# Gated mix of two attentions: 36 instead of 30 units on VectorE, seven operations each, and a bias column in ScalarE's exponential

## Chip, core and metric

The kernel runs on one core of a Trainium2 chip. The metric is the time of one execution on the device in microseconds; the time before is the median of three runs. Engines are named TensorE (PE), VectorE (DVE), ScalarE (ACT), GpSimd (POOL) and SyncE (SP) as in the profile.

## The reference

One sequence of 2048 tokens, 640 features, 32 heads of 20. Branch A is full softmax attention, branch B attends to 8 keys at distances 0, 2, ..., 14 back. A sigmoid gate of x mixes them. Both use the same x and have weights of their own.

```python
def _A_ref(x, wqkv, wo):            # 2048 keys for each query
    q, k, v = ...                   # 32 heads x 2048 x 20
    scores = einsum("bhqd,bhkd->bhqk", q, k) * 20 ** -0.5
    o = einsum("bhqk,bhkd->bhqd", softmax(scores), v)
    return merge_heads(o) @ wo

def _B_ref(x, wqkv, wo):            # 8 keys for each query
    kg, vg = k[..., idx, :], v[..., idx, :]     # idx = pos - 2 * (0..7)
    logits = einsum("bhsd,bhswd->bhsw", q, kg) * 20 ** -0.5
    attn = softmax(where(idx >= 0, logits, -1e9))
    o = einsum("bhsw,bhswd->bhsd", attn, vg)
    return merge_heads(o) @ wo

g = sigmoid((x * gate_w).sum(-1, keepdims=True))
return g * _A_ref(x, A_wqkv, A_wo) + (1 - g) * _B_ref(x, B_wqkv, B_wo)
```

Branch A has 32 x 2048 x 2048 exponentials, on 128 partitions 1,048,576 columns.

## The kernel before

**Units, steps and groups.** The work of branch A is cut into units of one head, one block of 128 keys (`kb`) and 512 queries: a score matmul of 32 rows into one PSUM bank of 128 x 512, an exponential, and a matmul with the values (`vA`, 21 columns, the first of which is one, so that the sum of the exponentials comes along). Four heads make a quad `q`, whose keys lie in `kT` and queries in `qT`, each head in 32 partitions. A quad and a block of 512 queries (`qc`) make a group of 64 units; there are 4 x 8 = 32 groups, numbered `gi`. Row 0 of each head's 32 is one in `kT` (from the column `e0`) and minus a bound on the scores in `qT` (`KM`, `qabs`), so the scores are already shifted when they come out of TensorE.

ScalarE takes its units in steps of three and two by turns, as wide as the PSUM banks 0 to 2 and 3 to 4 (`ST`): one instruction of 1536 or 1024 columns, line 1187, into one of six `ebuf`. Before it, TensorE has written the scores of the step (line 1172); after it, several steps' value matmuls run together (line 1195) into bank 5 (`OB`). At a group's end VectorE transposes that bank into `rg` (line 643) and normalizes it by the sums and the gate into `oTn` (lines 651 to 660).

**Units on VectorE.** A few units of each group (`XN`, at the places `XPOS`) never go to ScalarE. `gen_x` computes their exponential on VectorE, from a score matmul of its own (line 994): line 998 multiplies the score by `XMUL` and adds `XADD`, which makes a float whose integer value has the exponent of 2 in its upper bits; line 1002 clamps it and turns it into an integer; line 1003 takes the mantissa bits as a number between 1 and 2; lines 1004, 1006, 1007 and 1008 are a polynomial of it in the product form, and the last of them multiplies by the power of two that line 1005 cut out of the integer. `XADD` holds the logarithm of the polynomial's leading factor `XC4`. The three work tiles are `xb[0]`, `xb[1]` and `rg[0]`, the one that normalization uses, so a unit waits until the group before is normalized (`normdone`). Its result goes through a lone value matmul (line 1017) into bank 5.

**Other work.** The same five engines do all projections: keys (`gen_k`, line 412), queries (`gen_q`, lines 579 to 596, which first copies 80 columns of weights into `WqP`, line 382), values (`gen_v`). Branch B has three lanes: `gen_F` (lines 811 to 852) computes its queries, keys and products, `gen_K` (lines 866 to 966) its values, softmax and weighted sums, almost all on VectorE, with one small exponential on ScalarE per 512 queries (line 899); `gen_fold` and `gen_prefold` do the output projection. These lanes share the PSUM banks 6 and 7, which `take` and `give` hand around.

**What sets the order.** The order of the instructions on each engine is fixed when the program is built, by a planner at the end of `_build`. For each step `s` it places the step's exponential, the scores of step `s + 2`, the value matmuls when enough are pending, and in between pieces of the lanes. A lane is a generator that yields what it needs next ("pe", "dve", "dw" with a cost in ns, or "poll" until something holds); it has a window of steps in which it should proceed evenly, from `FWIN`, `KWIN`, `OWIN` in units of groups. A piece is placed if it fits into TensorE's and VectorE's planned time up to the step's end. A lane of group work that is not done in time is run to its end on the spot (`force`). Where TensorE would be left with little, filler matmuls are placed (lines 1314 and 1318). `task` records what each instruction reads and writes, and `emit` turns that into semaphore waits; each engine runs its list in order.

Of the kernel before, what the change touches and what calls it, by code (L numbers as in the profile page):

```python
# [5 lines left out]
FP32 = mybir.dt.float32  # L6
BF16 = mybir.dt.bfloat16
I32 = mybir.dt.int32
I16 = mybir.dt.int16
ALU = mybir.AluOpType  # L10
# [19 lines left out]
XC4 = 0.013534167746750096  # L30
XA = (-0.5785127719334512, 30.316837144955663, -17.76242689806009, 576.1803657752102)
XMUL = SCALE * 1.4426950408889634 * 2.0 ** 23
XADD = (127.0 + np.log2(XC4)) * 2.0 ** 23

XN = (0, 0, 1, 1, 1, 2, 2, 0, 1, 0, 0, 0, 0, 1, 2, 0, 0, 1, 1, 1, 1, 1, 0, 1, 2, 2, 1, 2, 1, 2, 1, 2)
FWIN = ((3.1, 4.4), (7.0, 11.7), (14.3, 18.8), (21.1, 25.7))
KWIN = ((6.3, 11.3), (6.0, 16.6), (15.3, 22.4), (24.3, 29.9))
OWIN = ((8.5, 12.7), (15.5, 20.2), (21.7, 25.8))
XPOS = ((7, 1), (9, 2), (5, 0))


class _Task:
# [202 lines left out]
def _build(ctx, nc, A_x, A_wqkv, A_wo, B_wqkv, B_wo, gate_w, out):  # L245
# [35 lines left out]
    zt = sb([P, P], BF16, "zt")  # L281
    Sel = sb([P, CN, 32], BF16, "Sel")
    e0 = sb([P, 1], FP32, "e0")
    KM = sb([P, NQUAD], BF16, "KM")
    Kmax = sb([P, 2, 5], FP32, "Kmax")
    WqP = [sb([P, CN, P], BF16, "WqP%d" % i) for i in range(2)]
    WkP = [sb([P, CN, P], BF16, "WkP%d" % i) for i in range(2)]
    kT = sb([P, NQUAD, S], BF16, "kT")
    vA = sb([P, NQUAD, KBN, 4 * VW], BF16, "vA")
    NQT = 3  # L290
    qT = [sb([P, 512], BF16, "qT%d" % i) for i in range(NQT)]
    qabs = sb([P, 512], BF16, "qabs")
    NEB = 6
# [2 lines left out]
    rr = [sb([P, 16], FP32, "rr%d" % i) for i in range(2)]  # L296
    rgn = [sb([P, 16, 32], BF16, "rgn")] * 2
    NOT = 14
    xb = [sb([P, 512], FP32, "xb%d" % i) for i in range(2)]
    oTn = sb([P, NOT, 512], BF16, "oTn")  # L300
    itmp = oTn[:, 10, 0:256].bitcast(I32)
    stmp = oTn[:, 11, 0:320].bitcast(I32).rearrange("p (c k) -> p c k", c=CN)
# [65 lines left out]
    T("pe", pe_warm, reads=["ident", "rgn"], writes=[("bk", 0)])  # L368
    T("dve", lambda e: e.memset(zt[:, :], 0.0), writes=["zt"])
    T("dve", lambda e: e.memset(e0[:, :], 0.0), writes=["e0"])  # L370
    for j in range(4):
        T("dve", lambda e, j=j: e.memset(e0[32 * j:32 * j + 1, :], 1.0), writes=["e0"])
    for i in range(2):
        T("dve", lambda e, i=i: e.memset(WkP[i][:, :, :], 0.0), writes=[("WkP", i)])
        T("dve", lambda e, i=i: e.memset(WqP[i][:, :, :], 0.0), writes=[("WqP", i)])

    T("dve", lambda e: e.memset(bank[OB], 0.0), writes=[("bk", OB)])

# [75 lines left out]
    def give(b, evac):  # L454
        held[b] = False
        if cur[0] is not None:
            cur[0].hold -= 1
        free_at[b] = evac.fin + 56.0
# [98 lines left out]

    def gen_q(gi):
        qc, q = divmod(gi, NQUAD)
        i = gi % 2  # L560
        yield ("dve", 370.0, 0.0)
        yield after(mk_wq(q, i))
        while ("KM", q) not in sch.bufs:
            yield ("poll",)
        b = yield from take()
        t = yield from chain(b, proj_mms(b, WqP[i], qc), [("WqP", i), "xT"])
        yield ("dw", t.fin, 690.0, 0.0)
        t = q_abs(b, gi)
        while ("KM", q) not in sch.bufs:
            yield ("poll",)  # L570
        yield ("t", max(t.fin, sch.bufs[("KM", q)][0].fin))
        yield ("pe", MM, 1.0)
        t = q_km(b, q)
        yield ("dw", t.fin, 690.0, 0.0)
        give(b, q_cp(b, gi))
# [402 lines left out]

    xdone = {}
    obstart = set()  # L980
    xA, xB, xC = xb[0], xb[1], rg[0]
    xe = xb[1][:, :].bitcast(BF16)[:, 0:512]

    def gen_x(gi, k, u):
        qc, q, kb, j = u
        while k > 0 and not xdone.get((gi, k - 1)):
            yield ("poll",)
        while gi > 0 and not normdone.get(gi - 1):
            yield ("poll",)
        A, B, C = xA[:, :], xB[:, :], xC[:, :]  # L990
        kA, kB_, kC = "xA", "xB", "rg"
        b = yield from take()
        yield ("pe", MM, 0.0)
        t = T("pe", lambda e: e.matmul(bank[b], kT[32 * j:32 * j + 32, q, kb * P:(kb + 1) * P], qT[gi % NQT][32 * j:32 * j + 32, :],  # L994
                                       start=True, stop=True),
              reads=[("kT", q, kb // 4), ("qT", gi % NQT)], writes=[("bk", b)], cost=MM)
        yield ("dw", t.fin, 690.0, 690.0)
        give(b, T("dve", lambda e: e.tensor_scalar(A, bank[b], float(XMUL), float(XADD), op0=ALU.mult, op1=ALU.add),  # L998
                  reads=[("bk", b)], writes=[kA], cost=690))
        Ai, Bi = A.bitcast(I32), B.bitcast(I32)  # L1000
        ops = [
            (430.0, lambda e: e.tensor_scalar(Ai, A, float(2 ** 23), None, op0=ALU.max), [kA], [kA]),
            (430.0, lambda e: e.tensor_scalar(Bi, Ai, 0x7FFFFF, 0x3F800000, op0=ALU.bitwise_and, op1=ALU.bitwise_or), [kA], [kB_]),
            (690.0, lambda e: e.scalar_tensor_tensor(C, B, XA[0], B, ALU.add, ALU.mult), [kB_], [kC]),
            (430.0, lambda e: e.tensor_scalar(Ai, Ai, 0x7F800000, None, op0=ALU.bitwise_and), [kA], [kA]),
            (690.0, lambda e: e.scalar_tensor_tensor(B, C, XA[2], B, ALU.add, ALU.add), [kC, kB_], [kB_]),
            (690.0, lambda e: e.scalar_tensor_tensor(C, C, XA[1], B, ALU.add, ALU.mult), [kB_, kC], [kC]),
            (690.0, lambda e: e.scalar_tensor_tensor(xe, C, XA[3], A, ALU.add, ALU.mult), [kA, kC], [kB_]),
        ]
        for c, fn, rd, w in ops:  # L1010
            yield ("dve", c, c)
            t = T("dve", fn, reads=rd, writes=w, cost=c)
        while (gi, j) not in obstart or (q, kb // 3) not in vdone:
            yield ("poll",)
        yield after(t)
        yield ("pe", MM, 0.0)
        T("pe", lambda e: e.matmul(bank[OB][32 * j:32 * j + DH + 1, :], vA[:, q, kb, VW * j:VW * j + DH + 1], xe, start=False,  # L1017
                                   stop=False, skip_group_check=True),
          reads=[kB_, ("vA", q, kb // 3)], accum=[("ob", j)], cost=MM)
        xdone[(gi, k)] = True  # L1020
# [163 lines left out]
    def mk_exp(s):  # L1184
        b0 = ST[s % 2][0]
        n = len(steps[s])
        return T("act", lambda e: e.activation(ebuf[s % NEB][:, 0:512 * n], ps[:, b0 * 512:(b0 + n) * 512], ACTF.Exp, scale=SCALE),  # L1187
                 reads=[("bk", b0 + i) for i in range(n)], writes=[("ebuf", s % NEB)], cost=ED[n])

    def mk_pv(s, us, cost):  # L1190

# [158 lines left out]
    for s in range(NS):  # L1350
# [4 lines left out]
        if first:  # L1355
            ng = gi + 1
            if ng < QCN * NQUAD:
                nqc, nq_ = divmod(ng, NQUAD)
                g_end = gstep(gi + 1)
                if nqc == 0:  # L1360
                    if nq_ % 2 == 1 and nq_ < NQUAD - 1:
                        p = (nq_ + 1) // 2
                        vl[p] = lane(gen_v(p), "v%d" % p, s + (20 if s == 0 else 2), gstep(gi + 2) + 8, 16.0)
                    ql[ng] = lane(gen_q(ng), "q%d" % ng, s + 4, g_end - 8 - lead(ng), 6.0, 2 if s == 0 else 1)
                else:
                    ql[ng] = lane(gen_q(ng), "q%d" % ng, s + 2, g_end - 10, 6.0, 0)
            n = len(xunits[gi])
            for k in range(n):
                sa, sb_ = s + 6, gstep(gi + 1) - 6
                xl[(gi, k)] = lane(gen_x(gi, k, xunits[gi][k]), "x%d.%d" % (gi, k), sa + k * (sb_ - sa) // n,  # L1370
                                   sa + (k + 1) * (sb_ - sa) // n, 4740.0, 0)
        E = mk_exp(s)
        odd = s % 2 == 1
        block[0], block[1] = False, 0.0
# [79 lines left out]
        while moved or not relaxed[0]:  # L1454
            relaxed[0] = not moved
            moved = False
            for g in sorted(lanes, key=lambda g: (g.hold == 0, g.s1 if g.name[0] in EAGER else INF)):
                if not g.done and g.due(s):
                    hot = g.name[0] in EAGER
                    lag = g.total * min(1.0, (s + 1 - g.s0) / max(1, g.s1 - g.s0)) - g.spent  # L1460
                    n = 0
                    while True:
                        lp = lim_pe
                        if npv[0] and not (hot and s >= g.s1):
                            lp = -INF
                        elif not hot and lag < 0.06 * g.total and block[1] >= SOFT:
                            lp = -INF
                        if not ready(g, s, lp, lim_dve):
                            break
                        moved = True  # L1470
                        n += 1
                        if not g.due(s) or (n >= 2 and not hot):
                            break
            for g in lanes:
                if g.done and not g.name.startswith("norm"):
                    ends.append((g.name, s, g.s1, round(g.spent, 1), g.total))
            lanes[:] = [g for g in lanes if not g.done]
# [65 lines left out]
```

## Time and profile before

| | |
|---|---|
| median of three runs | 949.87 us (949.42 to 951.07) |
| the profiled execution | 951.03 us |
| its span, first to last instruction | 949.2 us |
| mean granted TensorE clock | 0.996 |
| first exponential of line 1187 starts | 20.53 us |
| last one starts | 940.0 us |
| VectorE units: instructions of lines 998, 1002 to 1008 | 30 each, 141 us in all |
| normalization's transpose, line 643, waits for TensorE | 54.8 us |

The profile is one execution. Its busy times are the union of an engine's instructions, so overlapping instructions count once there, while the mean duration of a group is that of one instruction with its overlap. A line of the groups reads: line, engine, operation, output and inputs by name, shapes, count; then busy us and mean ns; then the idle time of the engine just before them, and what ended it. A row of the windows has, after the window and its length, the busy us of PE, its weight loads, DVE, ACT and POOL, with their counts, the granted TensorE clock, the DMA share and GB/s.

The span is a start of 20 us (loads, transposes of x, the first projections), the stream of exponentials of 921 us, and an end of 8 us with the last group's normalization and output.

### The profile page before, as it was taken

The numbers are of one execution on the slowest core, as the hardware profiler recorded it, in microseconds if no ns is written. First come the engines' busy times: TensorE is split into PE (matmuls) and PEld (weight loads), VectorE is DVE, ScalarE is ACT, GpSimd is POOL, SyncE is SP. The second block draws the span as 40 slices with busy tenths as digits, with TensorE's granted clock in tenths as the row PEclk, the third lists the DMA queues.
The fourth block names the chain that finished last, engine by engine and source line by source line (L and its number), as shares of the span: only waits on it lengthen the run. The fifth ranks groups of instructions, "written<-read, shape, count | busy, mean of one in ns | idle before, by whom it ended". The sixth has DMA issues, their size and how long they took to land.

```text
span 949.2 us, 16591 instructions
## 1 busy us (share of the span) xinstructions
PE 867.3 (91%) x6359; PEld 285.5 (30%) x6359; DVE 699.9 (74%) x1294; ACT 930.3 (98%) x833; POOL 3.1 (0%) x7
## 2 busy tenths in 40 slices
PE   8999999999889899999889899898899999899997
PEld 5333323232222222333222223322222333222232
DVE  5486665775688878668788876688898578898735
ACT  5999999999999999999999999999999999999997
POOL 1000000000000000000000000000000000000000
PEclk9999999999999999999999999999999999999999
DMA  9000000000000000000000000000000000000000
GB/s 311 9 1 20 17 1 1 1 22 15 1 1 2 1 1 1 1 15 8 8 1 1 1 1 8 9 14 1 1 2 1 8 9 15 1 2 1 1 1 29
DMA packets 12033, 12.86 MB, mean 14 GB/s; under 512 B 3380, under 2 KB 11316, under 8 KB 11956
## 3 DMA queue, kind: packets, MB, share of 16 engines
q1 hardware_dynamic: 9844, 11.43, 3.8%
q8 instruction: 52, 0.85, 0.4%
q10 hardware_dynamic: 2112, 0.37, 0.2%
q14 instruction: 25, 0.20, 0.1%
HBM read 9.18 MB, written 2.62 MB: 12 GB/s over the span
## 4 chain that ended last, share of the span: by engine, by line
ACT 68%; issue 16%; PE 15%; DVE 1%; DMA 1%; SPq 0%; ACTq 0%; DVEq 0%
ACT ebuf L1187 67%; PE ps L1172 5%; PE ps L400 4%; PE ps L1314 2%; PE ps L1195 2%; DMA x_tm<-in_A_x_dram 1%; PE ps L1039 1%; PE ps L483 0%; ACT L_sb L899 0%; PE ps L994 0%; DVE Kmax L1070 0%; PE ps L926 0%; PE ps L886 0%; PE ps L826 0%; PE ps L1017 0%
## 5 line engine op out<-in xcount | busy, mean ns | idle before, releaser
L1187 ACT ACTIVATE ebuf<-ps 128x1536 bf16<-128x1536 f32 (+1 forms) x807 | 915.6, 1358 | 2.2 <-PE ps L1172 1.0
L1172 PE MATMUL ps<-qT,kT 32*128 32x512 bf16 x2048 | 318.6, 382 | 66.0 <-ACT ebuf L1187 56.7
L1172 PEld LDWEIGHTS ps<-qT,kT 32*128 32x128 bf16 x2048 | 88.3, 91 | 345.5 <-issue 149.7
L1195 PE MATMUL ps<-ebuf,vA 128*21 128x512 bf16 x2018 | 170.7, 382 | 0.0
L1314 PE MATMUL ps<-xT,ident 128*128 128x512 bf16 x272 | 105.5, 388 | 6.7
L956 DVE TENSOR_TENSOR bw<-vB,bw 128x640 f32<-128x640 bf16 x112 | 91.9, 820 | 2.1
L960 DVE TENSOR_TENSOR blkacc<-blkacc,bw 128x640 f32<-128x640 f32 x96 | 78.9, 822 | 2.4
L842 DVE TENSOR_TENSOR prod<-qk 128x512 bf16<-128x512 bf16 x160 | 57.9, 418 | 15.8 <-PE ps L826 15.5
L1195 PEld LDWEIGHTS ps<-ebuf,vA 128*21 128x21 bf16 x2018 | 41.8, 90 | 72.3 <-issue 49.4
L400 PE MATMUL ps<-xT,WqkB 128*128 128x512 bf16 x200 | 63.5, 385 | 0.0
L643 DVE STREAM_TRANSPOSE rg<-ps 128x512 f32<-128x512 f32 x31 | 22.2, 717 | 54.8 <-PE ps L1195 54.8
L400 PE MATMUL ps<-woA_r,oTn 128*128 128x320 bf16 x240 | 48.5, 302 | 0.0
L1314 PEld LDWEIGHTS ps<-xT,ident 128*128 128x128 bf16 x272 | 26.0, 96 | 71.8 <-PE ps L1314 46.1
L400 PE MATMUL ps<-xT,WqP 128*128 128x512 bf16 (+1 forms) x165 | 47.2, 384 | 0.1
L400 PE MATMUL ps<-xT,WkP 128*128 128x512 bf16 (+1 forms) x165 | 46.1, 381 | 0.0
L579 DVE CAST qT<-ps 128x512 bf16<-128x512 f32 x31 | 21.4, 691 | 33.1 <-PE ps L400 33.0
L412 DVE TENSOR_SCALAR kT<-ps,e 128x512 bf16<-128x512 f32 x28 | 20.9, 748 | 28.8 <-PE ps L400 28.7
L400 PE MATMUL ps<-xT,WvB 128*128 128x512 bf16 x100 | 31.7, 384 | 0.0
L998 DVE TENSOR_SCALAR xb<-ps 128x512 f32<-128x512 f32 x30 | 20.7, 688 | 14.7 <-PE ps L994 9.9
L400 PE MATMUL ps<-WvA,oBacc 128*128 128x320 bf16 x160 | 31.3, 301 | 0.0
L596 DVE CAST qT<-ps 128x512 bf16<-128x512 f32 x31 | 21.3, 688 | 13.2 <-PE ps L589 13.1
L483 PE MATMUL ps<-WvA,xT 128*128 128x160 bf16 (+1 forms) x320 | 29.7, 233 | 0.0
(121 smaller groups left out, 653.0 us busy)
## 6 DMA issues: line engine op xcount, KB each, us to landing
x_tm<-in_A_x_dram SPq DMA_DIRECT2D x3, 640.0 KB
out_dram<-outsb SPq DMA_DIRECT2D x12, 160.0 KB
WqkB<-in_B_wqkv_dram SPq DMA_DIRECT2D x1, 1600.0 KB
WqkA<-in_A_wqkv_dram SPq DMA_DIRECT2D x2, 700.0 KB
qk<-in_B_wqkv_dram SPq DMA_DIRECT2D x1, 800.0 KB
woA_r<-in_A_wo_dram SPq DMA_DIRECT2D x32, 25.0 KB
WvA<-in_B_wo_dram SPq DMA_DIRECT2D x5, 160.0 KB
x_tm<-in_A_x_dram SPq DMA_DIRECT2D x2, 320.0 KB
```

The source lines that it names most:

```text
L400: ins = e.matmul(o, l, r, start=(k0 + k == 0), stop=(k0 + k == n - 1))
L483: ins = e.matmul(bank[b][:, i_ * wn:(i_ + 1) * wn], xT[:, c, kb * P:(kb + 1) * P], WvA[:, c, w0:w0 + wn], start=(c == 0), stop=(c == CN - 1))
L579: T("dve", lambda e: e.tensor_copy(qt[:, :], bank[b]), reads=[("bk", b)], writes=[("qT", gi % NQT)], cost=690)
L596: return T("dve", lambda e: e.tensor_copy(qT[gi % NQT][:, :], bank[b]), reads=[("bk", b)], writes=[("qT", gi % NQT)], cost=690)
L643: return T("dve", lambda e: e.transpose(rg[i][:, :], bank[OB]), reads=[("ob", j) for j in range(4)], writes=["rg"], cost=720)
L842: t = T("dve", lambda e, r=r, f=f, off=off: e.tensor_tensor(prod[r][:, :], qB[:, f, :], kB[:, f, off:off + 512], ALU.mult), reads=["qB", " ...
L956: T("dve", lambda e, vv=vv, av=av: e.tensor_tensor(tmpB, vv, av, ALU.mult), reads=[("aT", ai), "vB4"], writes=["tmpB"], cost=822)
L960: T("dve", lambda e: e.tensor_tensor(blkacc[:, :, :], blkacc[:, :, :], tmpB, ALU.add), reads=["tmpB"], writes=["blkacc"], cost=822)
L1172: ins = e.matmul(bank[b0 + i], kT[32 * j:32 * j + 32, q, kb * P:(kb + 1) * P], qT[gi % NQT][32 * j:32 * j + 32, :], start=True, stop=True)
L1187: return T("act", lambda e: e.activation(ebuf[s % NEB][:, 0:512 * n], ps[:, b0 * 512:(b0 + n) * 512], ACTF.Exp, scale=SCALE), reads=[("bk" ...
L1195: ins = e.matmul(bank[OB][32 * j:32 * j + DH + 1, :], vA[:, q, kb, VW * j:VW * j + DH + 1], ebuf[s % NEB][:, i * 512:(i + 1) * 512], start ...
L1314: T("pe", lambda e: e.matmul(bank[b], ident[:, :], xT[:, 0, 0:512], start=True, stop=True), reads=["xT", "ident"], writes=[("bk", b)], cos ...
```

## The change

It does seven things.

- The VectorE exponential has seven operations. The first one clamps the score from below at `XMIN` and multiplies it by `XMUL`, straight into an integer tile. Line 1002 goes. Without the addition the exponent's offset of 127 is missing; the mask that cuts out the exponent bits gets an exclusive-or with 0x40000000 as second operation, which puts it back up to a factor of two.
- The constant that `XADD` held is put on the other side: line 1187's exponential gets a bias, the column `xlog`, 128 x 1 in SBUF, filled with `ln(2 / XC4)`, so ScalarE's units carry the same factor as VectorE's; it cancels in the normalization.
- A third tile `xb[2]` takes the place of `rg[0]`. Room for it comes from `WqP` (one instead of two) and `qT` (two instead of three).
- A unit no longer waits for the previous group's normalization, but for all earlier units and for the end of its own group's query projection. Its lane's window begins seven steps before its group.
- `XN` has 36 units instead of 30, in other groups, up to three in one (`XPOS` has a fourth place).
- The windows of branch B's and the output's lanes are other numbers.
- In the planner's inner loop a lane of VectorE units ("x") or of `gen_K` ("K") gives way after each piece, so these two alternate.

```diff
-XADD = (127.0 + np.log2(XC4)) * 2.0 ** 23
-XN = (0, 0, 1, 1, 1, 2, 2, 0, 1, 0, 0, 0, 0, 1, 2, 0, 0, 1, 1, 1, 1, 1, 0, 1, 2, 2, 1, 2, 1, 2, 1, 2)
...
-XPOS = ((7, 1), (9, 2), (5, 0))
+XMIN = -126.0 / (SCALE * 1.4426950408889634)
+XLOG = float(np.log(2.0 / XC4))
+XN = (1, 2, 0, 2, 0, 2, 1, 2, 0, 0, 0, 0, 0, 1, 2, 1, 1, 0, 0, 3, 0, 2, 1, 1, 2, 2, 3, 1, 1, 1, 2, 2)
+FWIN = ((3.5, 2.1), (8.7, 7.6), (13.9, 21.4), (20.8, 24.3))
+KWIN = ((7.6, 8.5), (9.5, 12.4), (12.6, 24.7), (24.0, 23.4))
+OWIN = ((6.1, 13.1), (13.7, 23.5), (15.7, 31.2))
+XPOS = ((7, 1), (9, 2), (5, 0), (11, 3))
...
+    xlog = sb([P, 1], FP32, "xlog")
-    WqP = [sb([P, CN, P], BF16, "WqP%d" % i) for i in range(2)]
+    WqP = [sb([P, CN, P], BF16, "WqP")]
-    NQT = 3
+    NQT = 2
-    xb = [sb([P, 512], FP32, "xb%d" % i) for i in range(2)]
+    xb = [sb([P, 512], FP32, "xb%d" % i) for i in range(3)]
+    T("dve", lambda e: e.memset(xlog[:, :], XLOG), writes=["xlog"])
...
-    xA, xB, xC = xb[0], xb[1], rg[0]
+    xA, xB, xC = xb
-        while k > 0 and not xdone.get((gi, k - 1)):
+        while not all(xdone.get((g, i)) for g in range(gi + 1) for i in range(XN[g] if g < gi else k)):
-        while gi > 0 and not normdone.get(gi - 1):
+        while gi > 0 and not (gi in ql and ql[gi].done):
...
-        give(b, T("dve", lambda e: e.tensor_scalar(A, bank[b], float(XMUL), float(XADD), op0=ALU.mult, op1=ALU.add),
+        give(b, T("dve", lambda e: e.tensor_scalar(Ai, bank[b], float(XMIN), float(XMUL), op0=ALU.max, op1=ALU.mult),
-            (430.0, lambda e: e.tensor_scalar(Ai, A, float(2 ** 23), None, op0=ALU.max), [kA], [kA]),
-            (430.0, lambda e: e.tensor_scalar(Ai, Ai, 0x7F800000, None, op0=ALU.bitwise_and), [kA], [kA]),
+            (430.0, lambda e: e.tensor_scalar(Ai, Ai, 0x7F800000, 0x40000000, op0=ALU.bitwise_and, op1=ALU.bitwise_xor), [kA], [kA]),
...
-        return T("act", lambda e: e.activation(ebuf[s % NEB][:, 0:512 * n], ps[:, b0 * 512:(b0 + n) * 512], ACTF.Exp, scale=SCALE),
+        return T("act", lambda e: e.activation(ebuf[s % NEB][:, 0:512 * n], ps[:, b0 * 512:(b0 + n) * 512], ACTF.Exp, bias=xlog[:, 0:1],
+                                               scale=SCALE),
...
-                        if not g.due(s) or (n >= 2 and not hot):
+                        if not g.due(s) or (n >= 2 and not hot) or g.name[0] in "xK":
```

More of the change, by code (lines that the diff above doesn't have):

```diff
@@ L32 @@
 XMUL = SCALE * 1.4426950408889634 * 2.0 ** 23
-XADD = (127.0 + np.log2(XC4)) * 2.0 ** 23
-XN = (0, 0, 1, 1, 1, 2, 2, 0, 1, 0, 0, 0, 0, 1, 2, 0, 0, 1, 1, 1, 1, 1, 0, 1, 2, 2, 1, 2, 1, 2, 1, 2)
-FWIN = ((3.1, 4.4), (7.0, 11.7), (14.3, 18.8), (21.1, 25.7))
-KWIN = ((6.3, 11.3), (6.0, 16.6), (15.3, 22.4), (24.3, 29.9))
-OWIN = ((8.5, 12.7), (15.5, 20.2), (21.7, 25.8))
-XPOS = ((7, 1), (9, 2), (5, 0))
+XMIN = -126.0 / (SCALE * 1.4426950408889634)
[5 more added lines that the diff above has]
+XPOS = ((7, 1), (9, 2), (5, 0), (11, 3))
 class _Task:
@@ L374, in _build @@
         T("dve", lambda e, i=i: e.memset(WkP[i][:, :, :], 0.0), writes=[("WkP", i)])
-        T("dve", lambda e, i=i: e.memset(WqP[i][:, :, :], 0.0), writes=[("WqP", i)])
+    T("dve", lambda e: e.memset(WqP[0][:, :, :], 0.0), writes=[("WqP", 0)])
     T("dve", lambda e: e.memset(bank[OB], 0.0), writes=[("bk", OB)])
@@ L559, in gen_q @@
         qc, q = divmod(gi, NQUAD)
-        i = gi % 2
+        i = 0
         yield ("dve", 370.0, 0.0)
@@ L985, in gen_x @@
         qc, q, kb, j = u
-        while k > 0 and not xdone.get((gi, k - 1)):
+        while not all(xdone.get((g, i)) for g in range(gi + 1) for i in range(XN[g] if g < gi else k)):
             yield ("poll",)
-        while gi > 0 and not normdone.get(gi - 1):
+        while gi > 0 and not (gi in ql and ql[gi].done):
             yield ("poll",)
         A, B, C = xA[:, :], xB[:, :], xC[:, :]
-        kA, kB_, kC = "xA", "xB", "rg"
+        kA, kB_, kC = "xA", "xB", "xC"
         b = yield from take()
@@ L997, in gen_x @@
         yield ("dw", t.fin, 690.0, 690.0)
-        give(b, T("dve", lambda e: e.tensor_scalar(A, bank[b], float(XMUL), float(XADD), op0=ALU.mult, op1=ALU.add),
+        Ai, Bi = A.bitcast(I32), B.bitcast(I32)
+        give(b, T("dve", lambda e: e.tensor_scalar(Ai, bank[b], float(XMIN), float(XMUL), op0=ALU.max, op1=ALU.mult),
                   reads=[("bk", b)], writes=[kA], cost=690))
-        Ai, Bi = A.bitcast(I32), B.bitcast(I32)
         ops = [
-            (430.0, lambda e: e.tensor_scalar(Ai, A, float(2 ** 23), None, op0=ALU.max), [kA], [kA]),
             (430.0, lambda e: e.tensor_scalar(Bi, Ai, 0x7FFFFF, 0x3F800000, op0=ALU.bitwise_and, op1=ALU.bitwise_or), [kA], [kB_]),
             (690.0, lambda e: e.scalar_tensor_tensor(C, B, XA[0], B, ALU.add, ALU.mult), [kB_], [kC]),
-            (430.0, lambda e: e.tensor_scalar(Ai, Ai, 0x7F800000, None, op0=ALU.bitwise_and), [kA], [kA]),
+            (430.0, lambda e: e.tensor_scalar(Ai, Ai, 0x7F800000, 0x40000000, op0=ALU.bitwise_and, op1=ALU.bitwise_xor), [kA], [kA]),
             (690.0, lambda e: e.scalar_tensor_tensor(B, C, XA[2], B, ALU.add, ALU.add), [kC, kB_], [kB_]),
@@ L1186, in mk_exp @@
         n = len(steps[s])
-        return T("act", lambda e: e.activation(ebuf[s % NEB][:, 0:512 * n], ps[:, b0 * 512:(b0 + n) * 512], ACTF.Exp, scale=SCALE),
-                 reads=[("bk", b0 + i) for i in range(n)], writes=[("ebuf", s % NEB)], cost=ED[n])
+        return T("act", lambda e: e.activation(ebuf[s % NEB][:, 0:512 * n], ps[:, b0 * 512:(b0 + n) * 512], ACTF.Exp, bias=xlog[:, 0:1],
+                                               scale=SCALE),
+                 reads=[("bk", b0 + i) for i in range(n)] + ["xlog"], writes=[("ebuf", s % NEB)], cost=ED[n])
     def mk_pv(s, us, cost):
@@ L1366, in _build @@
                     ql[ng] = lane(gen_q(ng), "q%d" % ng, s + 2, g_end - 10, 6.0, 0)
[L1367 to L1371, printed above, removed]
+            for g_ in ((0, 1) if s == 0 else (gi + 1,)):
+                if g_ < QCN * NQUAD:
+                    n = len(xunits[g_])
+                    sa, sb_ = (6 if g_ == 0 else gstep(g_) - 7), gstep(g_ + 1) - 6
+                    for k in range(n):
+                        xl[(g_, k)] = lane(gen_x(g_, k, xunits[g_][k]), "x%d.%d" % (g_, k), sa + k * (sb_ - sa) // n,
+                                           sa + (k + 1) * (sb_ - sa) // n, 4310.0, 0)
         E = mk_exp(s)
```

## The prediction

> **What bounds the kernel now.** I read the busy table of the page first, then the groups by form, then the first microseconds of ScalarE's timeline, then TensorE's windows. The page:
>
> ```profile
> PE 867.3 (91%) x6359; PEld 285.5 (30%) x6359; DVE 699.9 (74%) x1294; ACT 930.3 (98%) x833; POOL 3.1 (0%) x7
> ...
> L1187 ACT ACTIVATE ebuf<-ps 128x1536 bf16<-128x1536 f32 (+1 forms) x807 | 915.6, 1358 | 2.2 <-PE ps L1172 1.0
> L1172 PE MATMUL ps<-qT,kT 32*128 32x512 bf16 x2048 | 318.6, 382 | 66.0 <-ACT ebuf L1187 56.7
> ```
>
> ScalarE is busy 98% of the span, 915.6 us of it in the 807 exponentials of line 1187, and it stood idle only 2.2 us in front of them. TensorE waits 56.7 us for those exponentials. So the end is set by one thing: the number of ScalarE exponentials times what each adds to an unbroken stream. VectorE (74%) is not on that path.
>
> ScalarE's groups by form:
>
> ```profile
> L1187 ACT ACTIVATE ebuf<-ps 128x1536 bf16<-128x1536 f32 x404 | 635.1, 1572 | 0.7 <-PE ps L1172 0.3
> L1187 ACT ACTIVATE ebuf<-ps 128x1024 bf16<-128x1024 f32 x403 | 461.1, 1144 | 1.5 <-PE ps L1172 0.7 <-ACT ebuf L1187 0.2
> ...
> L1066 ACT ACTIVATE kT<-ps,e 128x512 bf16<-128x512 f32 x3 | 2.1, 687 | 3.0 <-DVE Kmax L1070 2.3 <-PE ps L400 0.6
> ...
> L1049 ACT ACTIVATE xT<-ps 128x512 bf16<-128x512 bf16 x2 | 1.2, 594 | 1.4 <-PE ps L1039 1.4
> ```
>
> Two things stand here. 512 more columns cost 1572 - 1144 = 428 ns, 0.836 ns a column. And the inputs: line 1187 reads only ps, line 1066 reads ps and e, the bias column e0 in SBUF. At 512 columns the instruction with a bias column lasts 687 ns, the plain copy 594.
>
> **Part one: 30 units become 36.** A unit is one head, 128 keys, 512 queries. ScalarE keeps 2048 - 36 = 2012 units: in the changed program's instruction list 402 exponentials of 1536 columns and 403 of 1024, against 404 and 403. A duration is not what an exponential adds, since neighbours overlap (635.1 + 461.1 is more than 915.6). From the first exponential's start (20.53 us) to the last one's end (941.43) are 920.9 us; 2018 x 512 columns at 0.836 are 863.7, the four local softmax exponentials (line 899) about 3.4, which leaves 53.8 us over 812 activations, 66 ns each, the 2.2 us of idle included. So each 1536-wide exponential adds 1284 + 66 = 1350 ns, and two fewer give 2.7 us. This lies wholly on the path: -2.7.
>
> **Part two: a bias in the remaining 805.** Before, the bias of line 1187 is the number 0 inside the instruction; after, it is the column xlog in SBUF. No exponential of the trace has that, but line 1066 does, and once two of them follow each other directly. ScalarE's timeline there, and two plain copies in a row:
>
> ```profile
> 13.69 1.51 ACT L1049 ACTIVATE xT<-ps 128x1024 bf16<-128x1024 bf16 x2 [0.21 <-PE ps L1039]
> ...
> 18.58 1.05 ACT L1066 ACTIVATE kT<-ps,e 128x512 bf16<-128x512 f32 x2 [2.34 <-DVE Kmax L1070]
> ```
>
> In the trace's nanoseconds the copies run 13,691 to 14,715 (1024 columns) and 14,612 to 15,204 (512): the second one's end is 489 after the first one's, 61 more than its 428 of columns. With the bias column they run 18,578 to 19,265 (512) and 19,165 to 19,632 (256): 367 end to end, 153 more than its 214. The second was free to start: the VectorE reduction that it waits for ended at 18.82. The price is 153 - 61 = 92 ns by ends; by starts it is 159 (587 - 428) against 65 (921 - 856), 94. I take 93, since this is the nearest row: same engine, PSUM source, back to back, bf16 out. 805 x 93 = 74.9 us, with nothing to hide it, because ScalarE has no idle to give.
>
> Bounds for it: the lowest visible price compares Identity with the exponential itself, 687 - 428 = 259 fixed against 1043 - 856 = 187 for the first 1024-wide exponential, 72 ns, 58 us. The highest takes starts of the pair, 159, against the first two exponentials' starts (1331 - 1284 = 47), 112 ns, 90 us. Zero is a rival below.
>
> The Trainium skill speaks against this edit: ScalarE: Activation LUTs, section "What ACT_TABLE_LOAD costs", says that each per-partition pointer operand adds about 93 ns to an ACTIVATE. By that the sum is the same 74.9, and the pair above agrees; that exponentials in a long stream pay it is shown by no run here.
>
> **Part three: VectorE.** The first operation now clamps and multiplies PSUM into int32. No row has just that; line 998 (688 ns, PSUM to f32) and line 1002 (427, f32 to int32 in SBUF, as fast as line 1003's int32 to int32 at 424) bound a conversion at about nothing. Line 1002's operation goes, and the mask of line 1005 gets a second operation, for which 1003 with two (424) against 1005 with one (418) says +6. A unit costs 688 + 424 + 689 + 424 + 684 + 689 + 688 = 4.29 us instead of 4.71: 36 x 4.29 - 30 x 4.71 = +13 us of VectorE, under an engine with 249 us idle, stretched further by part two. On the path: 0; if the cover went it would be at most these 13. TensorE gets six more lone score and value matmuls; its 312 fillers (lines 1314, 1318) become 282, so it has room: 0.
>
> **Part four: waits and placement.** A third buffer lets a unit start before the previous group's normalization has read rg. One WqP and two qT instead of two and three: the copy into WqP (375 ns) waits for the projection one group, some 29 us, earlier, and qT's writer for scores two groups back, both long over. VectorE runs in order, so a unit whose score matmul is late holds up what stands behind it: projection copies, which feed qT, which feeds TensorE's next scores. That wait was 14.7 us over 30 units in front of line 998, 0.5 each, and it cost ScalarE nothing. The alternation with the local branch changes order only, and its work lies inside the same VectorE idle. 0, with a few us for the range. A memset for xlog and one fewer for WqP: 0.
>
> **Sum** against the profiled execution's span: 949.2 - 2.7 + 74.9 = 1021.4. What lies around the span was 1.8 us in that run (951.03); the median, 949.87, stands 0.7 over its span. So 1022.1 as a median; I say 1022.
>
> **Rivals.** First, the other side: the fetch of the bias column is hidden in a long stream, because the next exponential is issued while the last one runs (durations grow from 1457 for the first to 1572 on average with no change in pace, so the queue gets deeper). It decides if the whole 93 ns fits into that lead; then only part one is left, 949.87 - 2.7 = 947.2, faster. From about 3 ns exposed (2.7 us over 805) the change gains nothing. Against it: in the pair, which was free to overlap, neighbours overlap by 100 ns (19,265 - 19,165), the copies by 103, so the fetch was not absorbed. Chance 0.10.
>
> Second, TensorE's clock. TensorE's windows:
>
> ```profile
> 280.00:284.00 4.00, 2.47 (x19) 0.66 (x17) 3.90 (x7) 4.00 (x5) 0.00 (x0) 1.00 0.00 0
> 284.00:288.50 4.50, 4.50 (x20) 0.96 (x17) 2.04 (x4) 3.48 (x4) 0.00 (x0) 0.62 0.02 4
> ```
>
> After 4 us at 62% busy the granted clock fell to 0.62 of full in the next 4.5 us, and ScalarE lost 0.74 + 0.28 us of idle, about 1.4 with the late start. The Trainium skill, TensorE: Matmul & The Clock Gate, "Why this matters for your kernels", asks for idle gaps over about 3 us before the clock drops; by it nothing happens here. The row differs: the longest gap in that stretch was 0.92. A longer exponential thins TensorE's work by 8%. Cut into 3.4 us stretches, the length of the slowed one in the clock's records, the trace has TensorE below 0.78 busy in seven of 276 besides the start, and one of the seven was followed by the slow clock; six more at 1.4 us give 1022 + 8 = 1030. Chance of a loss of that kind, above 1026: 0.12.
>
> Third, VectorE's denser order leaves scores late: group 19 carries three units, 12.9 us in one 29 us group beside the local branch. One unit late by its own length costs 4.3 us; three, 13: 1035. For it: VectorE is busy 88 of 115 us between 487 and 602, where that group lies. Against it: between 602 and 717 it is busy 99 of 115 and ScalarE still all 115, and the slower stream gives 9 us more in such a stretch. Chance 0.03.
>
> **How the numbers follow.** Exposed price at about its size: 0.75, 1022, between 949.9 - 2.7 + 58 = 1005 and 949.9 - 2.7 + 90 = 1037. Hidden 0.10; clock 0.12; VectorE 0.03. The range 1006 to 1036 takes in nearly all but the hidden case. A change under 0.2% (1.9 us) can't be told from none here: faster 0.09, within 0.01 (a price of about 3 ns), slower 0.90.
>
> **What would show it.** Exponentials some 93 ns longer by pace: a pair of 1536 and 1024 taking about 2.45 us instead of 2.26 from end to end; ScalarE still 98% busy with about 990 us in the exponentials; the busy shares of TensorE and VectorE down to about 84% and 70%; TensorE's wait for ScalarE well above 56.7 us. If the pace stays at 2.26 the hidden rival holds and this forecast is wrong. If ScalarE's idle in front of its exponentials exceeds 5 us, clock windows or late VectorE work took it.

## The result and the profile after

The changed kernel takes 1023.25 us (median of four runs, 1019.07 to 1024.88) against 949.64 for the kernel before: 1.0767 times, 95% interval 1.0732 to 1.0802. The profiled execution took 1023.27 us with a span of 1021.5, 72.3 more than before. The ratios here and below leave out a single execution, of the kernel with a column of zeros, that took 3843.23 us where the others took 1021.

The busy table and the costliest groups of the changed kernel (line 1189 is the old 1187, line 1174 the old 1172):

```profile
PE 880.7 (86%) x6337; PEld 288.1 (28%) x6337; DVE 705.9 (69%) x1306; ACT 998.0 (98%) x831; POOL 3.1 (0%) x7
...
L1189 ACT ACTIVATE ebuf<-ps,xlog 128x1536 bf16<-128x1536 f32 (+1 forms) x805 | 984.1, 1501 | 7.8 <-PE ps L1174 7.5
L1174 PE MATMUL ps<-qT,kT 32*128 32x512 bf16 x2050 | 323.1, 386 | 126.5 <-ACT ebuf L1189 116.7
```

ScalarE is still the bound at 98%. It works 984.1 us for 805 exponentials where it worked 915.6 for 807, and TensorE waits twice as long for it (116.7 us, 56.7 before). The input list now reads ps,xlog. New is the end of that line: ScalarE stood idle 7.8 us in front of exponentials, 2.2 before, and nearly always until TensorE had written the scores.

ScalarE's groups by form:

```profile
L1189 ACT ACTIVATE ebuf<-ps,xlog 128x1536 bf16<-128x1536 f32 x402 | 689.2, 1714 | 2.5 <-PE ps L1174 2.4
L1189 ACT ACTIVATE ebuf<-ps,xlog 128x1024 bf16<-128x1024 f32 x403 | 518.3, 1287 | 5.2 <-PE ps L1174 5.1
```

An exponential lasts 142 or 143 ns more. That is not its price, as neighbours overlap. Eight of them in a row, four of each width, before and after, without a wait between them:

```profile
399.44 9.26 ACT L1187 ACTIVATE ebuf<-ps 128x1536 bf16<-128x1536 f32 x8
400.02 10.07 ACT L1189 ACTIVATE ebuf<-ps,xlog 128x1536 bf16<-128x1536 f32 x8
```

They take 0.81 us more, some 100 ns each, and the longer duration of the first is still in it. The price itself is read from end to end, over the whole trace: the median exponential of 1536 columns ends 1432 ns after the one before it, of 1024 columns 1005 ns; in the kernel before, 1344 and 917. So 88 ns each, 805 x 88 = 71 us. Less the columns, at 0.833 ns each, that is 152 ns now and 64 before.

The waits have a place. ScalarE's timeline and the windows at one of five such places:

```profile
326.62 9.11 ACT L1189 ACTIVATE ebuf<-ps,xlog 128x1536 bf16<-128x1536 f32 x7
336.55 1.11 ACT L1189 ACTIVATE ebuf<-ps,xlog 128x1024 bf16<-128x1024 f32 x1 [0.83 <-PE ps L1174]
338.49 1.54 ACT L1189 ACTIVATE ebuf<-ps,xlog 128x1536 bf16<-128x1536 f32 x1 [0.82 <-PE ps L1174]
```

```profile
329.50:333.00 3.50, 2.32 (x17) 0.70 (x17) 2.41 (x7) 3.50 (x4) 0.00 (x0) 1.00 0.00 0
333.00:340.00 7.00, 6.59 (x26) 1.34 (x25) 2.71 (x7) 5.35 (x5) 0.00 (x0) 0.51 0.00 0
```

In the first window TensorE is busy 2.32 of 3.5 us. In the next seven its granted clock is 0.51 of full: it is busy nearly throughout, and ScalarE, 5.35 of 7.0, waits for scores. The kernel before had one such stretch of 3.4 us after its start, this one has four of 6.8 and one of 3.4. All but 0.1 of the 7.8 us of idle lies in these five stretches or within 0.7 us behind them. The four runs go along with it: 1019.07 at a mean clock of 0.993, 1023.23 and 1023.27 at 0.986 and 0.985, 1024.88 at 0.983.

### The profile page after: what moved, and what is told of

Read it like the earlier page. It is cut to its first block, busy times and chain, and to the rows that moved or that the text cites. A ratio compares the mean times of both kernels' runs of the same rounds, so it can differ in the third digit from the quotient of the medians.

```text
span 1021.5 us, 16550 instructions
## 1 busy us (share of the span) xinstructions
PE 880.7 (86%) x6337; PEld 288.1 (28%) x6337; DVE 705.9 (69%) x1306; ACT 998.0 (98%) x831; POOL 3.1 (0%) x7
## 4 chain that ended last, share of the span: by engine, by line
ACT 67%; issue 18%; PE 12%; DMA 1%; DVE 1%; SPq 0%; ACTq 0%
ACT ebuf L1189 67%; PE ps L1174 4%; PE ps L403 4%; PE ps L1198 1%; PE ps L1317 1%; DMA x_tm<-in_A_x_dram 1%; ACT L_sb L902 0%; PE ps L1041 0%; PE ps L829 0%; PE ps L592 0%; PE ps L997 0%; PE ps L486 0%; PE ps L1019 0%; DVE Kmax L1072 0%; PE ps L737 0%
## 5 line engine op out<-in xcount | busy, mean ns | idle before, releaser
L1189 ACT ACTIVATE ebuf<-ps,xlog 128x1536 bf16<-128x1536 f32 (+1 forms) x805 | 984.1, 1501 | 7.8 <-PE ps L1174 7.5
L1174 PE MATMUL ps<-qT,kT 32*128 32x512 bf16 x2050 | 323.1, 386 | 126.5 <-ACT ebuf L1189 116.7
L1317 PE MATMUL ps<-xT,ident 128*128 128x512 bf16 x251 | 98.9, 395 | 6.5
L403 PE MATMUL ps<-woA_r,oTn 128*128 128x320 bf16 x240 | 51.4, 309 | 0.0
L1002 DVE TENSOR_SCALAR xb<-ps 128x512 int32<-128x512 f32 x36 | 24.8, 689 | 34.6 <-PE ps L997 23.2
L582 DVE CAST qT<-ps 128x512 bf16<-128x512 f32 x31 | 21.4, 691 | 32.1 <-PE ps L403 32.0
L814 DVE CAST qk<-ps 128x512 bf16<-128x512 f32 x40 | 27.4, 686 | 13.5 <-PE ps L403 13.2
L403 PE MATMUL ps<-xT,WvB 128*128 128x512 bf16 x100 | 36.4, 385 | 0.0
L877 DVE CAST vB<-ps 128x512 bf16<-128x512 f32 x20 | 13.8, 690 | 32.3 <-PE ps L403 32.0
L403 PE MATMUL ps<-WvA,oBacc 128*128 128x320 bf16 x160 | 34.4, 308 | 0.3 <-issue 0.3
```

The lines of the kernel that those rows point to most:

```text
L403: ins = e.matmul(o, l, r, start=(k0 + k == 0), stop=(k0 + k == n - 1))
L582: T("dve", lambda e: e.tensor_copy(qt[:, :], bank[b]), reads=[("bk", b)], writes=[("qT", gi % NQT)], cost=690)
L814: give(b, T("dve", lambda e, dst=dst, b=b: e.tensor_copy(dst, bank[b]), reads=[("bk", b)], writes=[key], cost=690))
L1002: give(b, T("dve", lambda e: e.tensor_scalar(Ai, bank[b], float(XMIN), float(XMUL), op0=ALU.max, op1=ALU.mult), reads=[("bk", b)], writes= ...
L1174: ins = e.matmul(bank[b0 + i], kT[32 * j:32 * j + 32, q, kb * P:(kb + 1) * P], qT[gi % NQT][32 * j:32 * j + 32, :], start=True, stop=True)
L1317: T("pe", lambda e: e.matmul(bank[b], ident[:, :], xT[:, 0, 0:512], start=True, stop=True), reads=["xT", "ident"], writes=[("bk", b)], cos ...
```

## The experiments

Two questions: is it the bias column alone that makes each exponential dearer; and where do the slow-clock stretches come from, and what do they cost? The diffs are shortened to the operations that change.

**One column of zeros in the kernel before.**

```diff
-  e.activation(ebuf..., ps..., ACTF.Exp, scale=SCALE)
+  e.activation(ebuf..., ps..., ACTF.Exp, bias=warm[:, 0:1], scale=SCALE)
```

> The kernel before with one edit: line 1187's bias is a column of zeros in SBUF instead of the number 0. Order of all instructions unchanged. If the bias column is what costs, at the 88 ns by which the changed kernel's pace shows it (152 against 64 ns beyond the columns): 949.6 + 807 x 0.088 = 1021. If instead the new placement of units and lanes costs the 73 us and the column is free in a stream: 950. For the slow-clock stretches of the changed kernel: if the slower pace of ScalarE brings them, some appear here too, clock 0.98 to 0.99 and up to 1026; if the new placement brings them, clock 0.996 and 1019 to 1021.

1020.73 to 1021.71 us, 1.0755 times (1.0737 to 1.0773). Its group of exponentials:

```profile
L1187 ACT ACTIVATE ebuf<-ps,warm 128x1536 bf16<-128x1536 f32 (+1 forms) x807 | 985.4, 1505 | 3.8 <-PE ps L1172 3.7
```

The count and the placement of before, and 985.4 us instead of 915.6. End to end it is again 152 ns beyond the columns. So the column by itself makes nearly all of the loss. Three slow stretches appear in the order of the kernel before, whose profile had one, and the clock is 0.993 in each of these executions, where the kernel before had 0.998 to 1.000 in the same comparison: the slower pace brings some of them.

**Two columns.** The scale too is read from SBUF.

```diff
+  e.activation(ebuf..., ps..., ACTF.Exp, bias=warm[:, 0:1], scale=xsc[:, 0:1])
```

> The kernel before with two columns, bias (zeros) and scale, in place of the two numbers of line 1187. If each fetch costs by itself: 949.6 + 2 x 807 x 0.088 = 1092. If both are fetched together at one price: 1021. If columns were free: 950.

1102.03 us (two executions), 1.1607 times (1.1584 to 1.1631).

```profile
L1189 ACT ACTIVATE ebuf<-ps,warm,xsc 128x1536 bf16<-128x1536 f32 (+1 forms) x807 | 1060.2, 1634 | 8.9 <-PE ps L1174 8.4
```

243 ns end to end beyond the columns: 64, 152, 243. Each column has its own price, 88 and 91 ns, and they are not paid for together. The time is 10 us above the expected 1092: ScalarE waits 8.9 us instead of 2.2, and the clock is down to 0.976 and 0.972.

**The change without the column.** The factor 2/XC4 can leave through the polynomial: a leading coefficient that is a power of two, and an argument at a quarter of its size (an or with 0x3E800000), so that the powers of two cancel. The polynomial's relative error, worked out from its constants, is then some 3e-5 instead of 3e-6.

```diff
-XA = (-0.5785127719334512, 30.316837144955663, -17.76242689806009, 576.1803657752102)
+XA = (0.009032874806456315, 0.7583040242659084, -0.027091328702227746, 0.26321644717503684)
-  tensor_scalar(Bi, Ai, 0x7FFFFF, 0x3F800000, bitwise_and, bitwise_or)
+  tensor_scalar(Bi, Ai, 0x7FFFFF, 0x3E800000, bitwise_and, bitwise_or)
-  ACTF.Exp, bias=xlog[:, 0:1], scale=SCALE
+  ACTF.Exp, scale=SCALE
```

> The changed kernel without the bias column. The constant goes into VectorE's polynomial instead: its leading coefficient is set to a power of two and its argument to a quarter, so the factor vanishes with no operation more. All else as in the changed kernel. If the bias column is the whole loss, only the two fewer exponentials are left: 949.6 - 2.7 = 947, pace 2.26 us for a pair, and a verdict of at best 0.3% faster. If placement loses, 955 to 1020. Slow-clock stretches: none or one if they come with the slower pace; several, and some 4 us on top (951), if they come with the placement.

953.73 us, 1.0041 times (1.0027 to 1.0055). A pair of exponentials takes 2.26 us again, as before. So 70 of the 73.6 us are gone with the column, and what is left is not a gain of 2.7 but a loss of 4.2. Group and windows:

```profile
L1186 ACT ACTIVATE ebuf<-ps 128x1536 bf16<-128x1536 f32 (+1 forms) x805 | 913.5, 1366 | 7.1 <-PE ps L1171 6.2 <-ACT ebuf L1186 0.2
```

```profile
308.00:311.40 3.40, 2.41 (x17) 0.62 (x17) 2.42 (x7) 3.40 (x4) 0.00 (x0) 1.00 0.00 0
311.40:318.10 6.70, 6.43 (x25) 1.35 (x25) 2.69 (x7) 4.79 (x5) 0.00 (x0) 0.50 0.00 0
```

The exponentials' 913.5 us are 2.1 under before, but ScalarE waits 7.1 us, 4.9 more. There are three slow stretches, at 110, 311 and 489 us. So the new placement has thin places of its own. In front of the one at 311 and of the one at 489 stands a group's end: TensorE may not write bank 5 until VectorE has transposed it. Whether that makes these places thin was not tried.

**The planner told of the price.** The changed kernel, column and all.

```diff
-    ED = {3: 1450.0, 2: 1025.0, 1: 600.0}
+    ED = {3: 1538.0, 2: 1113.0, 1: 688.0}
```

> The changed kernel with one edit: the planner's durations for an exponential (ED) are 88 ns longer, so it knows the price. It places 405 fillers instead of 282. If the slow-clock stretches come from a TensorE that the plan leaves too thin, the clock goes back to 0.995 and the time by 3 to 6 us to 1017 to 1020; ScalarE's idle in front of its exponentials falls from 7.8 to under 4 us. If they come from elsewhere, 1023 as before. The bias price stays: never below 1014.

1025.62 us, 1.0802 times (1.0786 to 1.0818): a miss in the time, not in the clock, which is 1.000 in the profiled run, without a slow stretch until the last microseconds. ScalarE's timeline tells why:

```profile
993.57 11.51 ACT L1189 ACTIVATE ebuf<-ps,xlog 128x1536 bf16<-128x1536 f32 x9
1011.25 2.12 ACT L1189 ACTIVATE ebuf<-ps,xlog 128x1024 bf16<-128x1024 f32 x2 [6.17 <-PE ps L1174]
```

With the longer exponentials the lane that projects the output of the last 512 queries was not done four steps before the end and was run there in one piece: 6.2 us of idle in one place. The rest of ScalarE's idle before exponentials is 2.1 us, down from 7.8. What the clock gave, this took.

**The price in the plan, and the old windows.** As the last one, with `FWIN`, `KWIN` and `OWIN` of the kernel before.

> The changed kernel, with the bias column, the planner told of 88 ns more per exponential, and the windows of the kernel before: 372 fillers, and no lane left for the end. The run with the price alone had the clock at 1.0 but 6 us of idle at one place near the end, where a lane had to be finished on the spot. If that was all that kept it at 1025: 1015 to 1018, clock 0.995 or more. If the slow clock had cost nothing in the changed kernel: 1022 to 1026.

1016.10 us, 1.0696 times (1.0674 to 1.0718).

```profile
L1189 ACT ACTIVATE ebuf<-ps,xlog 128x1536 bf16<-128x1536 f32 (+1 forms) x805 | 982.5, 1483 | 1.6 <-PE ps L1174 1.3
```

ScalarE waits 1.6 us instead of 7.8, and the median is 7 us lower. The pace is the same 152 ns. The windows make another order as well; but as the changed kernel's idle lay at its slow stretches, some 6 us of its loss were waits of the slow clock, and the rest is the column, less the two exponentials.

**More work at the thin places.** The kernel without the column, with score matmuls repeated.

```diff
+XD = (74, 75, 76, 200, 201, 202, 250, 251, 252, 403, 404, 405, 406, 504, 505, 506)
-            mk_qk(s + 2, again)
+            mk_qk(s + 2, again, 2 if s in XD else 0)
```

> The kernel without the bias column (953.7), with the same order on all engines, but in sixteen steps around the five places where the order gives TensorE least the score matmuls are issued three times over instead of once (some 80 more matmuls, the same result into the same banks). If ScalarE's loss there is the slow clock that follows a thin TensorE: clock at 0.995 or more, ScalarE's idle before its exponentials from 6.4 us to under 3, and 953.7 - 5 = 947 to 949. If VectorE's denser order is late by itself and the clock only goes along: the clock may rise, the time stays at 952 to 955.

950.42 us, 1.0009 times (0.9997 to 1.0021), clock 0.996. The windows are those of the same steps as the two shown for the kernel without the column (they lie 0.8 to 2.7 us earlier here):

```profile
306.60:310.65 4.05, 3.63 (x29) 0.88 (x27) 2.22 (x5) 3.82 (x4) 0.00 (x0) 1.00 0.00 0
310.65:315.40 4.75, 4.49 (x32) 1.37 (x32) 2.90 (x8) 4.70 (x5) 0.00 (x0) 1.00 0.00 0
```

TensorE is busy 3.63 of 4.05 us (90%) instead of 2.41 of 3.40 (71%), and the clock stays full after it. The first window got 0.65 us longer by the repeated matmuls, but the second takes 4.75 us instead of 6.7, for the same exponentials, ScalarE busy in all but 0.05 of it. VectorE's order is the same in both, so VectorE was not what was late. 3.3 of the 4.2 us are back, fewer than the five expected, and ScalarE's idle is 4.5 us, not under 3. The trace shows two reasons: repeated matmuls delay the scores by 0.2 to 0.4 us where the exponential before them is short, and two slow stretches of 3.4 us came at places that were not thickened, at 438 and 612 us.

**Repeats only where there is time for them.** 29 steps, each before a 1536-wide exponential.

> The kernel without the bias column with extra score matmuls again, but two fewer per place and only in steps whose successor on ScalarE is 1536 wide (29 steps, twice two more), where the scores have 1.35 us to be ready instead of 0.92. If the 200 to 400 ns by which ScalarE still waited at the thickened places came from the extra matmuls in the short steps: 946 to 948 with the clock at 0.995 or more, the first version faster than the kernel before. If the thin places need more work than that: slow clock again, 951 to 954.

950.06 us against 950.08 in the same comparison, 0.9999 times (0.9989 to 1.0010); the expected 946 to 948 were not reached. ScalarE's idle is down to 2.6 us:

```profile
L1187 ACT ACTIVATE ebuf<-ps 128x1536 bf16<-128x1536 f32 (+1 forms) x805 | 914.7, 1349 | 2.6 <-PE ps L1172 1.3 <-ACT ebuf L1187 0.2
```

Its stream of exponentials takes 920.2 us, 920.9 before. By its columns and its two fewer exponentials it should be 2.7 shorter; the other 2.0 went mostly into single exponentials that end 0.1 to 0.4 us late, of which only 0.4 us shows as idle. Its two runs with the clock at 1.000 took 948.56 and 948.62; the kernel before, in ten such runs of that comparison, 949.03 to 950.23. That would be a gain of some 1 us, from two runs. It is not shown: in the comparison of the run before this one, the kernel before took 948.55 to 949.55 at that clock.

**Other windows by plan.** 36 units without the column, with lane windows picked so that the planned work of TensorE had no thin place.

```diff
...
-KWIN = ((7.6, 8.5), (9.5, 12.4), (12.6, 24.7), (24.0, 23.4))
+KWIN = ((8.2, 9.1), (9.7, 12.2), (13.0, 24.9), (22.5, 23.7))
...
-    ED = {3: 1450.0, 2: 1025.0, 1: 600.0}
+    ED = {3: 1480.0, 2: 1055.0, 1: 600.0}
```

> 36 units, seven operations, no bias column, and other windows for the lanes of the local branch and the output, with the planner's exponentials 30 ns longer, chosen so that no three steps leave TensorE under 2.0 us of planned work (four such places without the bias column as it was): 348 fillers instead of 282. If the slow clock is what the placement lost, the gain of two fewer exponentials shows: 946 to 948, clock 0.996 or more. If the six more units cost by themselves on VectorE, 950 to 954.

954.95 us, 1.0049 times (1.0029 to 1.0068): a miss. Slow stretches came at 81, at 620 (10.2 us long) and at 805 us. Planned matmul time per step does not foretell a thin place well enough.

**The seven operations alone.** The kernel before with the shorter chain, constant in the polynomial, the old 30 units.

```diff
-  tensor_scalar(A, bank[b], XMUL, XADD, mult, add)
-  tensor_scalar(Ai, A, 2 ** 23, None, max)
+  tensor_scalar(Ai, bank[b], XMIN, XMUL, max, mult)
-  tensor_scalar(Ai, Ai, 0x7F800000, None, bitwise_and)
+  tensor_scalar(Ai, Ai, 0x7F800000, 0x40000000, bitwise_and, bitwise_xor)
```

> The kernel before with the seven operations alone: 30 units at the old places and windows, two work tiles and rg, no bias column, the constant in the polynomial. VectorE has 30 x 0.42 = 13 us less to do. If VectorE is off the path, nothing shows: 949.5 within 1. If its units hold up what sets the end, up to 3 us faster, 947.

951.82 us (949.33 to 956.24 over twelve runs), 1.0019 times (1.0002 to 1.0036). So 13 us less of VectorE bring nothing, as expected, but the median is 2.3 us above the 949.5, not within 1. Where the clock was 1.000 it took 949.33 to 950.33, the kernel before 948.55 to 949.55: the planner's changed order costs a little. The three runs near 956 have a clock of 0.992; the profiled one, 956.24, has slow stretches at 284 and 489 us.

> The run with the seven operations alone, whose times spread from 949.3 to 956.2, with the same extra matmuls at its 17 thin steps. If the spread is the phase of the clock's stretches against the thin places, it closes: all runs within 948 to 951, clock 0.996. If it is anything else, the spread stays.

With repeats at its thin steps all eleven runs lie between 951.45 and 953.67 at a clock of 0.998 or 1.000. The spread closes from 6.9 to 2.2 us together with the clock's; the level, 1.0020 times before (1.0010 to 1.0029), misses the expected 948 to 951. Even at a clock of 1.000 it takes 951.45 to 952.61, so here the repeats cost at least as much as they saved. In its trace three exponentials end 0.79, 0.37 and 0.37 us later than the usual pace. What delays the first was not tried; in front of the other two stand repeated matmuls.

## Why the prediction was right

The forecast was 1022 us, within 1006 to 1036; the measured median is 1023.25. Term by term:

- **Fewer units, -2.7 us.** The columns and the two exponentials are gone as counted. With the column removed the group's busy time is 2.1 under before (913.5 against 915.6). The gain never reached the end by itself: without the column the kernel was 4.2 us slower, because the placement that came with the six units brought slow-clock waits.
- **The column, 93 ns and 74.9 us.** Right in mechanism, a little large: 88 ns and 71 us, shown by the column of zeros alone. A pair takes 2.44 us, forecast 2.45. One pair of instructions in the first 20 us, and the care to compare ends with ends, gave the price of 805 others. The durations would have misled: they grew by 142 ns.
- **The hidden fetch** (0.10) fell. Of the 93 ns 88 showed in an unbroken stream, and a second column costs 91 again.
- **The clock** (0.12) was a part of what happened, not another case. It was priced at 8 us for six more stretches; four longer ones and one short one came, and ScalarE's idle rose by 5.6. The sign that the prediction named for it, idle above 5 us, showed: 7.8. That this term stood at zero in the sum is its real error. It was covered by the column being 4 us cheaper and the start of the stream 1.2 us earlier (19.3 against 20.5 us, which varies as much between the other runs' profiles). From end to end, exponentials that were late beyond the usual pace took 5.3 us more than before: -4.1 + 5.3 - 1.2 = 0.0, and the measured span is 0.1 above the forecast 1021.4. That the errors cancel so closely is luck.
- **From span to median.** The prediction put the median 0.7 us over the span, by setting the median of three runs against the span of another run. The profiled run lies 1.8 over its span, before and after; that is 1.1 of the 1.25 us between 1022 and the median.
- **Late VectorE work** (0.03) was not seen. A unit's seven operations took 689 + 422 + 680 + 415 + 681 + 683 + 683 = 4.25 us, forecast 4.29. The wait of the first one doubled from 0.5 to 1.0 us a unit (34.6 over 36), and ScalarE did not notice: where TensorE was kept busy, the time came back with VectorE's order unchanged.

The Trainium skill, ScalarE: Activation LUTs, "What ACT_TABLE_LOAD costs", gives about 93 ns for each per-partition pointer operand; the runs show 88 for the first and 91 for the second, in a stream of 800. The Trainium skill, TensorE: Matmul & The Clock Gate, "Why this matters for your kernels", asks for no idle gaps over some 3 us if the clock is to stay up. In the kernel before it fell after a stretch whose longest gap was 0.92, and with repeated score matmuls it stayed up at 311 us, where it had fallen in the same order without them, so the measurement decides against that rule as a bound.

## What to carry to other kernels

On an engine that is busy 98% of the time, the operands of its instruction are part of the price: a constant read from SBUF cost 7.5% here, one inside the instruction nothing, and here the constant could be moved into another engine's arithmetic. A price per instruction is best read from two neighbours of the right kind, end to end, wherever the trace has them. And a plan that thins a clocked engine's work can lose more through the clock than it gains in units, so look at the granted clock before blaming an engine's order.

## What the runs showed of the hardware

In the clock's records the slow clock is half of the full one and comes in stretches of 3.41 us or a multiple of it, up to 13.65 in the run with two columns. Over the twelve traces, cut into such stretches from 30 us on, it fell 29 times, each time after a stretch in which TensorE was busy 46 to 76% and its longest gap was 0.4 to 1.6 us. (Six of the traces lack about 100 of some 6400 matmul records, so their shares are a little low.) But many stretches were as thin and were not followed by a fall, in the changed kernel's complete trace 25 at 63 to 76%, so busy time alone does not decide it; what else does stays open. After 24 of the 27 slow stretches in which TensorE was busy without a break the clock came back; after 15 of the 20 at 81 to 98% it stayed slow, and so several lasted 6.8 us and more.
